# Attention followed by a gated MLP: natural token order for all batches at the gating step, one output store per token tile, and a divided last gating

## The chip, the cores and the metric

The kernel runs on one NeuronCore of a Trainium2 chip. The core has a matmul engine (TensorE, in profiles PE, with its weight loads as PEld), three engines for elementwise work (VectorE or DVE, ScalarE or ACT, GpSimd or POOL) and SyncE (SP), which here only issues DMAs. Each engine works through its own list of instructions in order and waits on semaphores for the others. The metric is the device time of one execution in microseconds (us). Before the change it was 246.58 us, the median of three runs (245.94 to 246.76).

## The reference

Eight batches of 384 tokens. First grouped-query attention: 16 query heads of 64 columns share 4 key and value heads. Its output, 384 x 1024 per batch, is the input of a gated MLP with a spatial part that mixes tokens. Cut to what matters:

```python
scores = matmul(q, k.T) / sqrt(64)           # per head, k and v repeated 4 times
x = softmax(scores) @ v                      # heads side by side: [8, 384, 1024]
h = maximum(x @ w_in, 0)                     # [8, 384, 1024]
u, v = h[..., :512], h[..., 512:]
v_n = (v - mean(v)) / sqrt(var(v) + 1e-6)    # per token
v_s = einsum('ts,bsd->btd', w_spatial, v_n) + b_spatial[None, :, None]
out = (u * v_s) @ w_out                      # [8, 384, 1024], float32
```

The product `u * v_s` is the gating; it is the step that the change touches.

## The kernel before

**Token orders.** Each batch has three token tiles (`NT = 3`) of 128. Queries are loaded so that one token is written as `c*12 + t*4 + r` (c of 32, t of 3, r of 4), and from the scores on the kernel's columns run in the order r, t, c within a tile; `units` (L254) turns the query columns with a rearrangement of its matmul's moving operand. So the attention output, and the MLP's activations after it, have their tokens in a permuted order: column `32*r + c` of tile t is token `c*12 + t*4 + r`. The spatial weights and bias are permuted to match when they are cast (`cast_spatial`, L527).

**Attention.** Per batch: `units` makes scores on PE and `exp` turns them into weights on ACT; `weigh` (L282) multiplies by v on PE, and DVE divides by the sums. A batch has six sets (query tile by head half), and a loop at the end of the kernel (L685 to L707) does one set per step. Keys, queries and attention outputs have to be transposed. In batches 0 and 1 PE does this; from batch 2 on SP issues DMA transposes: `k_send` and two `q_send` per batch (L237, L244), and one `x_send` per query tile (L324).

**MLP.** It is written as a generator, `gated` (L478), which the loop drains between attention's pieces (`pour`, L642), so that PE always has work. In a batch it makes `v_part` (v and its statistics), `norm` (POOL), `u_part`, then four times `s_part` (L416): three spatial matmuls into PSUM, a bias addition on DVE (`vs`, L433), and the gating product (`gT`). Output projection `o_part` (L450) of batch b stands in the generator of batch b+1: one call per token tile and half of 512 columns, four matmuls each, then a copy from PSUM to the tile `osb` on DVE or ACT. The last batch's six calls stand at the very end.

**Gating and stores before the change.** In batches 0 to 6, POOL multiplies in the permuted order (L435). In batch 7 the product is written with a stride, so that `gT` has the tokens in the order `token = 3*p + t` (L440): three on POOL, the fourth (`m == NM - 1`), which ends the wait of the last projection, on DVE. The stores follow: in batches 0 to 5 SP issues four DMAs after the third tile's second half, each from 32 partitions with all three tiles (L475); in batch 6 four per tile; in batch 7 one per tile and half from 128 partitions (L470). `osb` has two buffers of three tiles each.

**What sets the order.** Every engine's order is the order in which the program emits instructions (`manual_schedule`). Emission follows the loop: scores, part of the generator, the second half of the previous set's `weigh` with its `x_send`, more of the generator, the step's fixed tasks from `todo` (casts on POOL, `k_send`, `q_send`, loads), exponentials, and again the generator. SP therefore takes stores, transposes and loads strictly in that order, and each store waits at the head of SP's list until its copy is there. PSUM banks are given out by a planner that adds estimated costs (`bank`, `reads`); the change alters none of these costs.

**Set-up.** The spatial weights pass through a tile `early`, which takes a buffer of `osb`, and `ws16`, which takes one of `gT`. A `memset` on POOL (L581) overlaps both parts of `early`; SP's loads of the spatial weights and bias wait for it.

Of the kernel before, what the change touches and what calls it, by code (L numbers as in the profile page):

```python
# [9 lines left out]
FP32 = mybir.dt.float32  # L10
FP16 = mybir.dt.float16
AF = mybir.ActivationFunctionType
ALU = mybir.AluOpType
# [4 lines left out]
def kernel(  # L18
# [15 lines left out]
    P = 128  # L34
    B, HQ, S, D = q.shape
    HKV = k.shape[1]
    DM = moe_w_in.shape[0]
    DFF = moe_w_in.shape[1]
    DH = DFF // 2
    NT = S // P  # L40
    NK = DM // P
    NM = DH // P
    G = HQ // HKV
# [9 lines left out]
    cst = ctx.enter_context(tc.tile_pool(name="cst", bufs=1))  # L53
    ld = ctx.enter_context(tc.tile_pool(name="ld", bufs=2))
    att = ctx.enter_context(tc.tile_pool(name="att", bufs=2))
    moe = ctx.enter_context(tc.tile_pool(name="moe", bufs=2))
    small = ctx.enter_context(tc.tile_pool(name="small", bufs=4))
    ops = ctx.enter_context(tc.tile_pool(name="ops", bufs=2))
    ps = ctx.enter_context(tc.tile_pool(name="ps", bufs=1, space=PSUM))

    need = {AF.Exp, AF.Relu, AF.Copy, AF.Ln}
# [5 lines left out]
            name=nc.get_next_instruction_name(), act_func_set_id=set_id, ins=[], outs=[]  # L67
        )
    )
    pool, dve, act, sp = nc.gpsimd, nc.vector, nc.scalar, nc.sync  # L70
# [6 lines left out]
    def bank(shape, dtype, name):  # L77
        i = min(range(8), key=done.__getitem__)
        t = ps.tile(shape, dtype, name=name, tag=f"bank{i}")
        clock[nc.tensor] = max(clock[nc.tensor], done[i])  # L80
        done[i] = 1e12 + clock[nc.tensor]
        taken[name] = i
        return t

    def spend(ns):
        clock[nc.tensor] += ns

    def reads(eng, ns, name=None):
        clock[eng] = max(clock[eng], clock[nc.tensor] + 200.0) + ns
        if name:  # L90
            done[taken.pop(name)] = clock[eng]
# [60 lines left out]
    def load_w_in(half, lo, hi):  # L152
        cols = slice(half * DH, (half + 1) * DH)
        pool.dma_start(
            w_in16[:, lo:hi, cols],
            moe_w_in[lo * P : hi * P, cols].rearrange("(t p) f -> p t f", p=P),
        )
# [47 lines left out]
    def copy(eng, o, i, name):  # L205
        reads(eng, 200.0 + 0.52 * i.free_size(), name)
        (act.copy if eng is act else dve.tensor_copy)(o, i)  # L207
# [124 lines left out]
    v_r, v_n, mvs, uTs, gTs = {}, {}, {}, {}, {}  # L332
# [83 lines left out]
    def s_part(b, m):  # L416
        if m == 0:
            gTs[b] = moe.tile([P, NM, S], FP16, name=f"gT_{b}", tag="gT")
        psp = bank([P, 512], FP32, f"psp_{b}_{m}")
        for st in range(NT):  # L420
            nc.tensor.matmul(  # L421
                psp[:, 0:S],
                v_n[b, st][:, m * P : (m + 1) * P],
                wsT16[:, st, :],
                start=(st == 0),
                stop=(st == NT - 1),
            )
            spend(C384)
            if st < NT - 1:
                yield C384  # L430
        reads(dve, 470.0, f"psp_{b}_{m}")
        vs = moe.tile([P, S], FP32, name=f"vs_{b}_{m}", tag="vs", bufs=4)
        dve.tensor_tensor(vs, psp[:, 0:S], bias_bc, ALU.add)  # L433
        if b < B - 1:
            pool.tensor_tensor(gTs[b][:, m, :], vs, uTs[b][:, m, :], ALU.mult)  # L435
        else:
            def rows(x):
                return x.rearrange("p (o t c) -> p o t c", t=NT, o=G)

            (dve if m == NM - 1 else pool).tensor_tensor(  # L440
                gTs[b][:, m].rearrange("p (t c o) -> p o t c", t=NT, o=G),
                rows(vs),
                rows(uTs[b][:, m]),
                ALU.mult,
            )
        yield C384

    osbs = {}

    def o_part(b, tt, half):  # L450
        last = b == B - 1
        if tt == 0 and half == 0:
            osbs[b] = ops.tile([P, NT, DM], FP32, name=f"osb_{b}", tag="osb")
        po = bank([P, 512], FP32, f"po_{b}_{tt}_{half}")
        for m in range(NM):
            nc.tensor.matmul(  # L456
                po,
                gTs[b][:, m, tt * P : (tt + 1) * P],
                w_out16[:, m, half * 512 : (half + 1) * 512],
                start=(m == 0),  # L460
                stop=(m == NM - 1),
            )
            spend(C512)
            if m < NM - 1:
                yield C512
        cols = slice(half * 512, (half + 1) * 512)
        osb = osbs[b][:, tt, cols]
        copy(act if half and (last or tt == 1) else dve, osb, po, f"po_{b}_{tt}_{half}")
        if last:
            sp.dma_start(out[b].rearrange("(p t) d -> p t d", t=NT)[:, tt, cols], osb)  # L470
        elif half and (tt == NT - 1 or b == B - 2):
            ts = slice(tt, tt + 1) if b == B - 2 else slice(0, NT)
            rows = out[b].rearrange("(c t r) d -> r c t d", t=NT, r=G)
            for r in range(G):
                sp.dma_start(rows[r][:, ts], osbs[b][32 * r : 32 * r + 32, ts])  # L475
        yield C512

    def gated():  # L478
        for b in range(B):
            u0 = b * UNITS  # L480
            behind = [(b - 1, tt, half) for tt in range(NT) for half in range(2)] if b else []
            if b == 0:
                for st in range(NT):
                    yield ("from", 6 * st + 7)
                    yield from v_part(b, st, 0, 4)
                    yield ("from", 6 * st + 10)
                    yield from v_part(b, st, 4, 8)
            else:
                yield ("from", u0 + 12)
                yield from v_part(b, 0)  # L490
                for _ in range(1 if b == B - 1 else 2):
                    yield from o_part(*behind.pop(0))
                yield ("from", u0 + 18)
                yield from v_part(b, 1)
                yield ("from", u0 + 24)
                yield from v_part(b, 2)
# [9 lines left out]
            for m in range(NM):  # L506
                if behind:
                    yield from o_part(*behind.pop(0))
                yield from s_part(b, m)
            if behind:  # L510
                yield from o_part(*behind.pop(0))
# [2 lines left out]
                yield from o_part(B - 1, tt, half)  # L514


    early = ops.tile([P, NT, DM], FP32, name="early", tag="osb")
    ws32, b32 = early[:, :, 0:S], early[:, 0, S : 2 * S]
    ws16 = moe.tile([P, NT, NT, P], FP16, name="ws16", tag="gT")

    def load_spatial(eng):
        eng.dma_start(b32, moe_b_spatial.rearrange("(a s) -> a s", a=1).to_broadcast([P, S]))
        rows = moe_w_spatial.rearrange("(c t r) s -> r c t s", t=NT, r=G)
        for r in range(G):
            eng.dma_start(ws32[32 * r : 32 * r + 32], rows[r])
# [52 lines left out]
    load_v(1, pool)  # L578
    load_w_in(0, 0, 4)
    load_w_in(0, 4, 8)  # L580
    pool.memset(early[:, 0, S - 1 : S + 1], 0.0)  # L581
    load_spatial(sp)
    cast_k(1, pool)
    load_k(2, pool)
# [159 lines left out]
```

## Time and profile before

The profiled execution took 246.05 us; the runs' median is 246.58.

| | before |
|---|---|
| profiled execution, its own time | 246.05 us |
| span, first to last instruction | 244.3 us |
| granted TensorE clock, mean | 0.998 |
| PE busy | 234.9 us, 96% |
| ACT busy | 170.2 us, 70% |
| DVE busy | 144.9 us, 59% |
| POOL busy | 97.6 us, 40% |
| hardware DMA queue q1, share of 16 engines | 72.6% |
| output stores of L475, 384 KB | 24, median 6.3 us from issue to landing |
| output stores of L475, 128 KB | 12, median 2.1 us |
| output stores of L470, 256 KB | 6, median 2.8 us |
| gating on POOL, permuted order (L435) | 28, 912 ns (median) |
| gating on POOL, strided (L440) | 3, 1,059 ns |
| gating on DVE, strided (L440) | 1, 1,014 ns |

How to read it: "busy" is the time in which an engine executes; successive matmuls overlap and their ends are modelled, so a busy PE need not be at its peak rate, and two matmuls that follow one another start closer together than one lasts. `L456` is a line of the kernel. In a timeline, each line has start, duration, engine, line, operation and operands (out <- in), and in brackets how long the engine was idle before it and what ended that. SPq is SP's queue: the duration of a DMA there is that of its issue, not of its transfer. A waits line gives the waiting engine and line, who released it, then the total in us, the number of waits and the longest.

### The profile page before, as it was taken

The page shows a single profiled execution, that of the slowest core. Times are in us where ns is not written, and L with a number is a line of the kernel's source. Part 1 is how long each engine was busy: PE and PEld are TensorE (multiplying, and loading weights), DVE is VectorE, ACT ScalarE, POOL GpSimd, SP SyncE. Part 2 cuts the span into 40 slices and gives each one's busy share as a digit, 9 for nine tenths or more (in the row PEclk, how much of TensorE's full clock was granted, in tenths as well). Part 3 has the DMA queues.
Part 4 walks back from the last instruction along what each step waited for, and adds up shares of the span by engine and source line. Part 5 has one row for each costly group of instructions (what it writes and reads, how often), then busy time and mean ns, then how long its engine had stood idle before and what let it go on. Part 6 is the DMA issues. An engine that isn't in the chain of part 4 may idle for free.

```text
span 244.3 us, 5957 instructions
## 1 busy us (share of the span) xinstructions
PE 234.9 (96%) x2352; PEld 127.0 (52%) x2352; DVE 144.9 (59%) x377; ACT 170.2 (70%) x348; POOL 97.6 (40%) x137
## 2 busy tenths in 40 slices
PE   7899999999999999999999999899999999999992
PEld 6555565554555455555455455455455455545540
DVE  2677676567536765465844677266734767366371
ACT  2899977787898678968698776887597776402211
POOL 2677964545043900367024800466022400450520
PEclk9999999999999999999999999999999999999999
DMA  6999999992799999978999599987992297228267
GB/s 161 306 307 317 284 326 157 152 328 78 90 171 344 190 171 205 301 152 177 159 160 369 121 217 161 238 278 142 200 170 43 43 214 92 43 55 207 66 175 274
DMA packets 62411, 46.68 MB, mean 191 GB/s; under 512 B 45232, under 2 KB 54512, under 8 KB 62384
## 3 DMA queue, kind: packets, MB, share of 16 engines
q1 hardware_dynamic: 58560, 38.32, 72.6%
q0 software_dynamic: 3680, 7.87, 12.6%
q8 instruction: 18, 0.29, 0.5%
q10 hardware_dynamic: 144, 0.13, 0.3%
q14 instruction: 9, 0.07, 0.1%
HBM read 25.95 MB, written 12.58 MB: 158 GB/s over the span
## 4 chain that ended last, share of the span: by engine, by line
PE 74%; DMA 11%; SPq 8%; DVE 4%; issue 1%; ACT 0%; DVEq 0%
PE po L456 15%; PE pu L402 13%; PE pv L343 13%; PE sc L268 12%; PE av L288 12%; PE psp L421 7%; DMA wsT<-ws 5%; DMA qT<-q 5%; SPq L475 4%; SPq L239 3%; DMA k_None<-in_k_dram 1%; PE qps L229 1%; PE xps L320 1%; DVE x L303 1%; SPq L327 1%
## 5 line engine op out<-in xcount | busy, mean ns | idle before, releaser
L280 ACT ACTIVATE aT<-sc 128x512 f16<-128x512 f32 x288 | 147.7, 612 | 35.4 <-PE sc L268 34.7
L288 PEld LDWEIGHTS <-aT 128*128 128x128 f16 x1152 | 47.7, 97 | 17.7 <-issue 2.5
L288 PE MATMUL av<-v,aT 128*128 128x65 f16 x1152 | 51.7, 193 | 0.4 <-DVE osb L207 0.2
L343 PE MATMUL pv<-w_in,xt 128*128 128x512 f16 x192 | 51.3, 379 | 0.0
L456 PE MATMUL po<-w_out,gT 128*128 128x512 f16 x192 | 50.8, 379 | 0.4 <-DVE gT L440 0.4
L387 POOL TENSOR_SCALAR vn<-vr,rstd,nmr 128x512 f16<-128x512 f32 x24 | 18.1, 768 | 82.1 <-DVE nmr L382 60.3
L402 PE MATMUL pu<-xt,w_in 128*128 128x384 f16 x256 | 49.9, 326 | 0.0
L268 PE MATMUL sc<-qT,kT 64*128 64x512 f16 x288 | 42.7, 380 | 1.8 <-DMA qT<-q 1.2
L301 DVE RECIPROCAL r<-av 128x4 f32<-128x4 f32 x96 | 17.2, 179 | 43.4 <-PE av L288 43.2
L303 DVE TENSOR_TENSOR x<-av,r 128x256 f16<-128x256 f32 x96 | 40.8, 425 | 3.6 <-DVE r L301 0.4
L435 POOL TENSOR_TENSOR gT<-vs,uT 128x384 f16<-128x384 f32 x28 | 25.5, 914 | 29.5 <-DVE vs L433 15.0
L207 DVE COPY osb<-po 128x512 f32<-128x512 f32 x38 | 26.2, 689 | 17.4 <-PE po L456 17.2
L402 PEld LDWEIGHTS <-w_in 128*128 128x128 f16 x256 | 22.0, 97 | 17.1 <-issue 5.5
L413 ACT ACTIVATE uT<-pu 128x384 f16<-128x384 f32 x32 | 15.8, 494 | 17.1 <-PE pu L402 17.0
L456 PEld LDWEIGHTS <-gT 128*128 128x128 f16 x192 | 17.1, 97 | 17.9 <-issue 3.1
L268 PEld LDWEIGHTS <-kT 64*128 64x128 f16 x288 | 11.4, 94 | 26.2 <-issue 15.0
L343 PEld LDWEIGHTS <-xt 128*128 128x128 f16 x192 | 16.1, 97 | 17.3 <-issue 4.9
L194 POOL CAST q<-q 128x768 f16<-128x768 f32 x28 | 22.3, 827 | 6.8 <-DMA q<-in_q_dram 3.1
L421 PE MATMUL psp<-wsT,vn 128*128 128x384 f16 x96 | 22.3, 326 | 0.3 <-DMA wsT<-ws 0.3
L357 DVE TENSOR_SCALAR vr<-pv 128x512 f32<-128x512 f32 x24 | 16.4, 683 | 9.6 <-PE pv L343 9.5
L433 DVE TENSOR_TENSOR vs<-psp,bias_bc 128x384 f32<-128x384 f32 x32 | 17.6, 551 | 6.3 <-PE psp L421 4.8
L369 DVE BATCH_NORM_STATS2 stats<-vr 128x6 f32<-128x512 f32 x24 | 16.4, 685 | 0.1
(42 smaller groups left out, 102.8 us busy)
## 6 DMA issues: line engine op xcount, KB each, us to landing
out_dram<-osb SPq DMA_DIRECT2D x24, 384.0 KB, 6.3
q<-in_q_dram SPq DMA_DIRECT2D x10, 768.0 KB, 7.3
q<-in_q_dram POOLq DMA_DIRECT2D x4, 768.0 KB, 10.8
v_None<-in_v_dram SPq DMA_DIRECT2D x6, 384.0 KB, 4.6
w_in<-in_moe_w_in_dram POOLq DMA_DIRECT2D x4, 512.0 KB, 11.4
k_None<-in_k_dram SPq DMA_DIRECT2D x5, 384.0 KB, 4.0
out_dram<-osb SPq DMA_DIRECT2D x12, 128.0 KB, 2.1
out_dram<-osb SPq DMA_DIRECT2D x6, 256.0 KB, 2.8
```

The costliest lines, as they stand in the source:

```text
L194: eng.tensor_copy(t16[:, :, :, hh, :], src[:, hh])
L207: (act.copy if eng is act else dve.tensor_copy)(o, i)
L268: nc.tensor.matmul(sc, kTs[b][rows, j, kt * P : (kt + 1) * P], qTs[b, j][rows, qt].rearrange("p (r i c) -> p i r c", r=G, i=G), start=True ...
L280: act.activation(a, sc, AF.Exp, scale=scale)
L288: nc.tensor.matmul(av[:, i * (D + 1) : (i + 1) * (D + 1)], aT[:, kt, hh, i * P : (i + 1) * P], v1[b % 2][:, 2 * j + hh, kt, 0 : D + 1], st ...
L303: dve.tensor_tensor(x16s[b][:, qt, c : c + 256].rearrange("p (i d) -> p i d", i=G), o[:, :, 0:D], r.to_broadcast([P, G, D]), ALU.mult,)
L343: nc.tensor.matmul(pv, xts[b][:, kt, st * P : (st + 1) * P], w_in16[:, kt, DH:DFF], start=(kt == 0), stop=(kt == NK - 1),)
L387: pool.tensor_scalar(vn, v_r.pop((b, st)), rstd[:, st : st + 1], nmr[:, st : st + 1], op0=ALU.mult, op1=ALU.add,)
L402: nc.tensor.matmul(pu[:, 0:S], w_in16[:, kt, m * P : (m + 1) * P], xts[b][:, kt, :], start=(kt == 0), stop=(kt == NK - 1),)
L421: nc.tensor.matmul(psp[:, 0:S], v_n[b, st][:, m * P : (m + 1) * P], wsT16[:, st, :], start=(st == 0), stop=(st == NT - 1),)
L435: pool.tensor_tensor(gTs[b][:, m, :], vs, uTs[b][:, m, :], ALU.mult)
L456: nc.tensor.matmul(po, gTs[b][:, m, tt * P : (tt + 1) * P], w_out16[:, m, half * 512 : (half + 1) * 512], start=(m == 0), stop=(m == NM - 1),)
```

## The change

In every batch the gating product is now written in the strided form, so that `gT` has the natural order `token = 3*p + t` everywhere. With that, each token tile's output rows lie one per partition over all 128 partitions, and `o_part` issues one store per token tile (512 KB, rows of 4 KB) right after its second half, in batches 0 to 6 alike. Batch 7's stores stay one per tile and half. `osb` becomes one tile of `[128, 1024]` per token tile, with three buffers in all.

The last gating of batch 7 is divided: DVE writes the first token tile's 128 columns, POOL the other 256.

`early` is gone: the spatial weights, the bias and `ws16` get constant tiles of their own, and POOL has two memsets in place of one.

```diff
-    ops = ctx.enter_context(tc.tile_pool(name="ops", bufs=2))
+    ops = ctx.enter_context(tc.tile_pool(name="ops", bufs=3))
...
         dve.tensor_tensor(vs, psp[:, 0:S], bias_bc, ALU.add)
-        if b < B - 1:
-            pool.tensor_tensor(gTs[b][:, m, :], vs, uTs[b][:, m, :], ALU.mult)
+
+        gT = gTs[b][:, m].rearrange("p (t c o) -> p o t c", t=NT, o=G)
+        vs, uT = (x.rearrange("p (o t c) -> p o t c", t=NT, o=G) for x in (vs, uTs[b][:, m]))
+        if b < B - 1 or m < NM - 1:
+            pool.tensor_tensor(gT, vs, uT, ALU.mult)
         else:
-            def rows(x):
-                return x.rearrange("p (o t c) -> p o t c", t=NT, o=G)
-
-            (dve if m == NM - 1 else pool).tensor_tensor(
-                gTs[b][:, m].rearrange("p (t c o) -> p o t c", t=NT, o=G),
-                rows(vs),
-                rows(uTs[b][:, m]),
-                ALU.mult,
-            )
+            for eng, t in ((dve, slice(0, 1)), (pool, slice(1, NT))):
+                eng.tensor_tensor(gT[:, :, t], vs[:, :, t], uT[:, :, t], ALU.mult)
...
-        if tt == 0 and half == 0:
-            osbs[b] = ops.tile([P, NT, DM], FP32, name=f"osb_{b}", tag="osb")
+        if half == 0:
+            osbs[b, tt] = ops.tile([P, DM], FP32, name=f"osb_{b}_{tt}", tag="osb")
+        osb = osbs[b, tt]
...
-        osb = osbs[b][:, tt, cols]
-        copy(act if half and (last or tt == 1) else dve, osb, po, f"po_{b}_{tt}_{half}")
+        rows = out[b].rearrange("(p t) d -> p t d", t=NT)
+        copy(act if half and (last or tt == 1) else dve, osb[:, cols], po, f"po_{b}_{tt}_{half}")
         if last:
-            sp.dma_start(out[b].rearrange("(p t) d -> p t d", t=NT)[:, tt, cols], osb)
-        elif half and (tt == NT - 1 or b == B - 2):
-            ts = slice(tt, tt + 1) if b == B - 2 else slice(0, NT)
-            rows = out[b].rearrange("(c t r) d -> r c t d", t=NT, r=G)
-            for r in range(G):
-                sp.dma_start(rows[r][:, ts], osbs[b][32 * r : 32 * r + 32, ts])
+            sp.dma_start(rows[:, tt, cols], osb[:, cols])
+        elif half:
+            sp.dma_start(rows[:, tt, :], osb)
...
-    early = ops.tile([P, NT, DM], FP32, name="early", tag="osb")
-    ws32, b32 = early[:, :, 0:S], early[:, 0, S : 2 * S]
-    ws16 = moe.tile([P, NT, NT, P], FP16, name="ws16", tag="gT")
+    b32 = cst.tile([P, S], FP32, name="b32")
+    ws32 = cst.tile([P, NT, S], FP32, name="ws32")
+    ws16 = cst.tile([P, NT, NT, P], FP16, name="ws16")
...
-    pool.memset(early[:, 0, S - 1 : S + 1], 0.0)
+    pool.memset(b32[:, 0:1], 0.0)
+    pool.memset(ws32[:, 0, 0:1], 0.0)
```

## The prediction

> **What bounds the kernel now.** I read the busy table, PE's waits, the neighbourhood of each wait in the timeline, and last the DMA traffic of the tail.
>
> The busy table (engine, busy us, share of the span) and PE's own waits (us in total, times, longest):
>
> ```profile
> PE 234.9 (96%) x2352; PEld 127.0 (52%) x2352; DVE 144.9 (59%) x377; ACT 170.2 (70%) x348; POOL 97.6 (40%) x137
> ...
> PE sc L268 <- DMA qT<-q: 1.2, 2, 0.8
> ...
> PE po L456 <- DVE gT L440: 0.4, 1, 0.4
> ```
>
> PE is the bound; at a granted clock of 0.998 it can be helped only where it waits, and after its last matmul (235.22 + 4.71 = 239.93 of 244.3 us). Of its waits, the change can touch these two.
>
> First wait. The timeline of SP's queue, then of PE, around 139 to 154 us (start, us taken):
>
> ```profile
> 137.41 1.78 SPq L327 DMA_TRANSPOSE xt<-x  x1
> 139.29 4.60 SPq L475 DMA_DIRECT2D out_dram<-osb  x4
> 144.00 4.02 SPq L239 DMA_TRANSPOSE kT<-k  x1
> 148.13 4.11 SPq L246 DMA_TRANSPOSE qT<-q  x2
> ...
> 151.52 1.46 PE L402 MATMUL pu<-xt,w_in 128*128 128x384 f16 x8
> 153.79 0.39 PE L268 MATMUL sc<-qT,kT 64*128 64x512 f16 x2 [0.80 <-DMA qT<-q]
> ```
>
> Four stores hold SP for 4.6 us, the k transpose behind them takes 4.0 instead of the 1.2 to 1.5 it takes at 90.38 and 119.59, and q lands 5.6 us after its issue: PE waits. The same sequence stands 27.5 us later (wait 0.36 at 181.36).
>
> Second wait and the tail. DVE, PE and SP at the end, then the landing of the last batch's six stores:
>
> ```profile
> 234.15 1.01 DVE L440 TENSOR_TENSOR gT<-vs,uT 128x384 f16<-128x384 f32 x1
> 234.96 1.38 DVE L207 COPY osb<-po 128x512 f32<-128x512 f32 x2
> ...
> 233.17 1.67 PE L456 MATMUL po<-w_out,gT 128*128 128x512 f16 x7
> 235.22 4.71 PE L456 MATMUL po<-w_out,gT 128*128 128x512 f16 x21 [0.37 <-DVE gT L440]
> ...
> 229.55 7.86 SPq L475 DMA_DIRECT2D out_dram<-osb  x12
> 237.51 3.48 SPq L470 DMA_DIRECT2D out_dram<-osb  x6
> ...
> L470 SPq DMA_DIRECT2D out_dram<-osb x6: 376/400/581, 237.5 to 240.6; - x6
> DMA to landing us min/median/max: 2.5/2.8/3.0
> ```
>
> And the traffic of three windows: 218.1 to 222 (only 32-partition stores), 236.5 to 239 (batch 6's last 32-partition stores, then the first of batch 7) and 239.2 to 243 (only 128-partition stores):
>
> ```profile
> DMA packets 208, 0.80 MB, mean 206 GB/s; under 512 B 16, under 2 KB 16, under 8 KB 206
> ...
> DMA packets 223, 0.59 MB, mean 236 GB/s; under 512 B 63, under 2 KB 63, under 8 KB 223
> ...
> DMA packets 790, 1.42 MB, mean 374 GB/s; under 512 B 96, under 2 KB 96, under 8 KB 790
> ```
>
> The reader should see that stores from 32 partitions move 206 GB/s and stores from 128 partitions 374, and that from 236.5 to 243 the queue never empties: the last store, issued at 240.57, lands 2.8 us later, behind the ones before it.
>
> **The change, part by part.**
>
> *Stores of batches 0 to 5.* 24 issues of 384 KB become 18 of 512 KB. Their price on the engines that issue and move them is unknown, so bounds: issue between 0.40 us (128 rows of 2 KB, L470) and 0.67 (the first of a burst of four), take 0.55; transfer between 0.52 MB / 206 = 2.5 us and 0.52 / 374 = 1.4, take 1.4, because the row with 128 partitions is the nearer one. Where each goes in SP's order follows from PE's order: the third tile's store stays where the four were, behind an x transpose and ahead of the k transpose; the second tile's falls between two x transposes, where SP waits for DVE (5.9 us before 137.41) and its copy (ACT, done at 133.63) is long over; the first tile's comes after or between the two q transposes and ahead of an x transpose. Queued behind its wait there are an x transpose, needed about a batch later, and loads for two batches ahead; only batch 1's, near 87, falls ahead of k and q transposes, whose data are wanted at 100.9. So ahead of the k transpose 4.6 us and 1.57 MB become 0.55 us and 0.52 MB. From 139.29: store to 139.85, k transpose 1.2 to 1.5 to 141.4, first q transpose issued there, landing in 4.0 to 5.6: 147 at the latest, wanted at 152.8. Both waits go, with 5 us to spare; even 206 GB/s would cost only 1.1 of it. What each is worth: the eighth pu starts at 152.98 - 0.33 = 152.65, the next matmul could start one step (0.16) later, 152.82; 153.79 is 0.97 late, of which about 0.10 is the usual change to a score matmul (148.13 to 148.39 is 0.26). So 0.87; likewise 181.36 - (179.70 + 1.30 - 0.33 + 0.16) - 0.10 = 0.43. **Minus 1.3 us.** Nothing is late next there: the batches that start at 100.9 and 125.8 run the same work and show no such wait.
>
> *Gating written with a stride, batches 0 to 6.* 28 POOL instructions go from 912 to 1,059 ns (the three strided ones of L440): 4.1 us of POOL, which is 40% busy. Tightest cover: batch 6's last gating, 217.54 to 218.45, would end at 218.60, and its weights load at 218.69. The casts behind gatings in POOL's queue come 0.15 to 0.3 later; the one for the second q ends at 139.33, and its transpose would not be wanted before 142.5. Cost 0; without the cover at most 0.15 per batch.
>
> *Last gating divided.* It delays PE: the matmul before the wait starts at 233.17 + 1.67 - 0.38 = 234.46, the next could at 234.68 and does at 235.22: 0.54 late. DVE keeps 128 of 384 columns. Lower bound a third of 1,014, 338 ns; upper: DVE's plain products (256 columns 425, 384 columns 551) give 172 + 0.98 per column, so 298 ns, plus all of the 463 that the strided one costs more as if fixed, 760. I take the excess as per column: 298 + 154 = 452. Ready at 234.60, the 0.05 until PE follows included before 234.68: **minus 0.54** (0.26 at 760 ns). POOL's 256 columns, two thirds of 1,059 = 0.71, from 234.17 to 234.9, are wanted first by the second token tile at about 236.4: hidden.
>
> *Tail stores.* Batch 6's 12 issues become 3. Its last tile is copied 0.5 earlier, so its store goes at about 235.2 (235.70 now), moves in 1.4 instead of 2.2 us, and SP is free for batch 7's first store at once, where now four issues run until 237.42. All 2.1 MB at 374 GB/s take 5.6 us instead of 6.4 from the first packet on. The last store then hardly queues. Its landing by rows: 128 KB stores land in 1.9 at least, 0.35 to 0.64 of it transfer, so 1.4 fixed; 256 KB take 0.7 more: 2.1 in place of 2.8. **Minus 0.7** (bounds 0 and 0.8).
>
> *Three output buffers of one tile.* The copy of batch 7's third tile (239.10 now, 238.56 then) must wait for batch 6's third store: issued 235.2, 1.4 fixed + 1.4 = 238.0. Cost 0; at 206 GB/s it lands at 239.1, and the last issue comes 0.2 later.
>
> *Own tiles for the spatial weights.* A second memset, at most 0.155 us, ahead of loads that are issued from 16.60 to 19.63 and land in 7.1 and 8.8 (medians); POOL uses them from 28.71 and 29.51. Cost 0; with the cover gone 0.15, at the matmul that waits 0.3 for wsT.
>
> Sum: -1.3 - 0.54 - 0.7 = -2.5 us against the profiled execution: span 244.3 to 241.8, its own time 246.05 (span plus 1.75) to 243.5. The median of the runs, 246.58, is 0.53 above that execution; carried to it, **244.1 us**.
>
> **The rivals.**
>
> *POOL's piece holds up DVE's.* Both halves have two SBUF inputs. If they cannot run at once and POOL starts first, DVE's 128 columns begin at 234.17 + 0.71 and are ready at 235.33, 0.16 after today's 235.17: PE loses 0.16 instead of winning 0.54. 244.8 us. For it: nothing in the trace overlaps two such instructions, and POOL starts 0.08 to 0.14 after vs, DVE 0.10, nearly a tie. Against: DVE's L433 takes its 0.55 beside POOL's L440 all the same (230.79 beside 230.07), but it reads PSUM. If DVE starts first, POOL ends at 235.3, which is still hidden. The Trainium skill, page "SBUF — State Buffer", section "Who interferes with whom", says that such a VectorE instruction and a GpSimd one that reads SBUF exclude each other for their whole length; by that rule the halves never overlap, and the sum would be 244.1 or 244.8 by who starts first. No run here shows it yet. Chance 0.2.
>
> *The 128-partition store of whole rows moves only 206 GB/s.* Then batch 6's last one moves in 2.5 instead of 2.2 us, from 0.5 earlier, and batch 7's six follow without a gap as now: the end wins 0.2 instead of 1.24, 245.1. For it: its rows are 4 KB like those of the slow ones. Against: 374 with 128 partitions. Chance 0.1.
>
> *The transposes stay late,* held by something that the stores hide now (a cast on POOL, the release of a buffer): then 1.3 is missing, 245.4. Against: at 119.59 to 124.3 the same three need 4.7 us of SP in all. Chance 0.12.
>
> *Slower: too few output buffers.* Batch 7's third copy waits for batch 6's third store. If that lands at L, the copy takes 0.7, two issues 0.4 each follow, and the last lands 2.1 later: L + 3.4. That beats all that the middle wins (243.37 + 1.3) from L = 241.3, a landing of 6.1 us. 384 KB stores have taken up to 8.3 in this trace: L = 243.5, 248.8 us. Against: those ran among transposes, and none is left here. Chance 0.08.
>
> **Numbers.** Forecast 0.5. Range 243.2 to 245.8: below, the forecast's bounds (0.1 more in the tail, 0.1 in the landing of the waits) and the runs' spread (245.94 to 246.76); above, the transposes staying late with some of that spread. 0.3% (0.74 us) is about what a measurement tells from no change. Forecast, the first two rivals and most of the third are faster by more: 0.84; same 0.07; slower 0.09.
>
> **What would show it.** SP: one store of about 0.55 us ahead of each k transpose, k transposes of 1.2 to 1.5, and no wait of PE for qT. DVE's strided product near 0.45 us, beginning beside POOL's and not after it, and PE's 28 last matmuls without a gap. Traffic near 374 GB/s in every store, last landing about 2.1. It is wrong if PE waits for qT again, if a copy waits for out_dram near the end, or if POOL's longer products appear among PE's releasers.

## The result and the profile after

The changed kernel took 243.77 us (median of six runs), the kernel before 246.36 in six runs; the ratio is 0.9891 with a 95% interval of 0.9874 to 0.9908, so it is 1.1% faster. One of the six, 247.67 us, was slower than the rest at a lower granted clock (0.993) and is not in the ratio. Forecast were 244.1 us and a range of 243.2 to 245.8. The profiled execution took 243.88 us with a span of 241.8, the span that the sum had given. Outside the span lie 2.0 us, against 1.75 before.

The busy table after, and under it all of PE's waits (total us, times, longest):

```profile
PE 234.9 (97%) x2352; PEld 127.0 (53%) x2352; DVE 143.9 (60%) x377; ACT 169.8 (70%) x348; POOL 100.8 (42%) x139
...
PE idle L552 <- POOL ident masks.py:199: 1.4, 1, 1.4
PE qps L229 <- DVE q L197: 0.5, 1, 0.5
PE sc L268 <- DVE qT L207: 0.4, 2, 0.3
```

PE's work is the same 234.9 us. What is gone are its waits for qT and for the last gating, and two smaller ones that stood in the same list before:

```profile
PE psp L421 <- DMA wsT<-ws: 0.3, 1, 0.3
PE av L288 <- DVE osb L207: 0.2, 1, 0.2
```

POOL has 3.2 us more.

SP's queue at the place where the first wait arose, then PE where the score matmul had waited 0.80 us:

```profile
137.18 1.90 SPq L327 DMA_TRANSPOSE xt<-x  x1
139.17 0.53 SPq L469 DMA_DIRECT2D out_dram<-osb  x1
139.81 1.49 SPq L239 DMA_TRANSPOSE kT<-k  x1
141.39 3.35 SPq L246 DMA_TRANSPOSE qT<-q  x2
144.83 0.86 SPq L469 DMA_DIRECT2D out_dram<-osb  x1
...
151.29 1.46 PE L402 MATMUL pu<-xt,w_in 128*128 128x384 f16 x8
152.69 0.82 PE L268 MATMUL sc<-qT,kT 64*128 64x512 f16 x6
```

One store of 0.53 us stands ahead of the k transpose, which takes 1.49; the first q transpose goes out 6.7 us earlier than before, and the score matmul starts without a wait.

The tail: the last gating in its two parts, PE behind it, SP, and the landing of the six last stores:

```profile
232.62 0.45 DVE L441 TENSOR_TENSOR gT<-vs,uT 128x128 f16<-128x128 f32 x1
232.66 0.88 POOL L441 TENSOR_TENSOR gT<-vs,uT 128x256 f16<-128x256 f32 x1 [0.33 <-DVE vs L433]
...
231.64 6.21 PE L453 MATMUL po<-w_out,gT 128*128 128x512 f16 x28
...
233.61 0.33 SPq L469 DMA_DIRECT2D out_dram<-osb  x1
234.29 4.54 SPq L467 DMA_DIRECT2D out_dram<-osb  x6
...
L467 SPq DMA_DIRECT2D out_dram<-osb x6: 332/332/333, 234.3 to 238.5; - x6
DMA to landing us min/median/max: 2.0/2.2/2.7
```

All 28 matmuls of the last projections run without a gap. The last store, issued at 238.50, lands after 2.0 us; the prediction had taken 2.1 for one that does not queue.

To see where the 2.4 us came from, I cut each span at points that all kernels have: the first score matmul of batches 2, 4 and 7, the last spatial matmul, the start of the last projection matmul, the issue of the last store, the moment SP sees it landed, the end. Durations in us, from the start times in the traces:

| stage | before | after | difference |
|---|---|---|---|
| set-up, batches 0 and 1 | 51.56 | 51.60 | +0.04 |
| batches 2, 3 | 49.32 | 49.12 | -0.20 |
| batches 4 to 6 | 80.49 | 79.10 | -1.39 |
| batch 7 to the last spatial matmul | 51.65 | 51.66 | +0.01 |
| to the last projection matmul | 6.54 | 5.99 | -0.55 |
| to the issue of the last store | 1.03 | 1.03 | 0 |
| to its landing, seen by SP | 2.80 | 2.03 | -0.77 |
| to the end | 0.90 | 1.32 | +0.42 |

In the profiles of the experiments the stages from batch 2 to the last spatial matmul repeat within 0.1 us where the kernels do not differ there; the first one varies from 50.6 to 52.6 us without a relation to the edits that I could see. That is the scatter of the runs, and the reason why effects of half a microsecond are read below from the stages and not from the medians alone.

### The profile page after: what moved, and what is told of

It reads as the page before. It is cut to its first block, busy times and chain, and to the rows that moved or that the text cites. A ratio compares the mean times of both kernels' runs of the same rounds, so it can differ in the third digit from the quotient of the medians.

```text
span 241.8 us, 5961 instructions
## 1 busy us (share of the span) xinstructions
PE 234.9 (97%) x2352; PEld 127.0 (53%) x2352; DVE 143.9 (60%) x377; ACT 169.8 (70%) x348; POOL 100.8 (42%) x139
## 4 chain that ended last, share of the span: by engine, by line
PE 94%; DVE 3%; issue 0%; ACT 0%; POOL 0%; POOLq 0%
PE pu L402 18%; PE po L453 18%; PE pv L343 17%; PE sc L268 16%; PE av L288 15%; PE psp L421 7%; PE idle L552 2%; PE xps L320 1%; PE qps L229 1%; DVE x L303 1%; DVE vr L357 1%; PE kps L215 1%; DVE qT L207 1%; DVE q L197 0%; DVE r L301 0%
## 5 line engine op out<-in xcount | busy, mean ns | idle before, releaser
L453 PE MATMUL po<-w_out,gT 128*128 128x512 f16 x192 | 50.6, 379 | 0.0
L438 POOL TENSOR_TENSOR gT<-vs,uT 128x384 f16<-128x384 f32 x31 | 32.5, 1059 | 33.4 <-DVE vs L433 16.9
L268 PEld LDWEIGHTS <-kT 64*128 64x128 f16 x288 | 10.9, 94 | 24.9 <-issue 13.9
L433 DVE TENSOR_TENSOR vs<-psp,bias_bc 128x384 f32<-128x384 f32 x32 | 17.6, 552 | 6.5 <-PE psp L421 6.3
```

Of the source, the lines that this page charges most:

```text
L268: nc.tensor.matmul(sc, kTs[b][rows, j, kt * P : (kt + 1) * P], qTs[b, j][rows, qt].rearrange("p (r i c) -> p i r c", r=G, i=G), start=True ...
L438: pool.tensor_tensor(gT, vs, uT, ALU.mult)
L453: nc.tensor.matmul(po, gTs[b][:, m, tt * P : (tt + 1) * P], w_out16[:, m, half * 512 : (half + 1) * 512], start=(m == 0), stop=(m == NM - 1),)
```

## The experiments

**1. The division undone.** The changed kernel, DVE doing the whole last gating:

```diff
-            for eng, t in ((dve, slice(0, 1)), (pool, slice(1, NT))):
+            for eng, t in ((dve, slice(0, NT)),):
```

> The changed kernel with the last gating undivided again: DVE writes all 384 columns. Theory (the division is worth its 0.54 us because the last store no longer queues): the product takes about 1.01 us, PE's last projection shows a gap again whose matmul comes 0.5 us late, the last landing moves by as much, 0.45 to 0.6 us more than the changed kernel (243.8), about 244.3. Rival (the end is set by the queue of output stores, not by PE): the gap returns but the last landing does not move, 243.8.

Measured: 244.26 us (six runs, 244.09 to 244.58), 0.49 more than the changed kernel. PE's gap is back:

```profile
PE po L453 <- DVE gT L441: 0.4, 1, 0.4
```

The two kernels did not run at the same time, and their ratios to the kernel before, 0.9899 (0.9861 to 0.9936) here and 0.9891, do not tell them apart. The stages do: the one to the last projection matmul is 6.54 again, 0.55 more, and landing and end are as in the changed kernel (2.03 and 1.34). The theory holds: with the queue gone, PE's half microsecond reaches the end in full.

**2. The division alone.** The kernel before, with the last gating of batch 7 divided:

```diff
-            (dve if m == NM - 1 else pool).tensor_tensor(
+            parts = ((pool, slice(0, NT)),)
+            if m == NM - 1:
+                parts = ((dve, slice(0, 1)), (pool, slice(1, NT)))
+            for eng, t in parts:
...
```

> The kernel before with nothing but the last gating of batch 7 divided between DVE (first token tile) and POOL. Theory: PE's gap of 0.37 us before the last projection goes; batch 6's last stores start 0.5 us earlier and the queue of stores moves with them, so 0.5 us less than before (246.4), about 245.9; the last store still lands 2.8 us after its issue and the two waits for qT (0.8 and 0.4) stay. Rival (the queue of stores alone sets the end): PE ends 0.5 us earlier, but the last landing only 0 to 0.2, 246.2 to 246.4.

Measured: 245.55 us in twelve runs beside 246.48 of before, ratio 0.9956 (0.9932 to 0.9979). The stage to the last projection matmul is 5.99, the last store needs 2.78 us to land as before, and the waits for qT stay:

```profile
PE sc L268 <- DMA qT<-q: 1.2, 2, 0.8
```

So the queue of stores moves forward with PE and does not eat the gain; the rival falls.

**3. The tail's stores alone.** The kernel before, with batch 6 in the natural order and one store per token tile:

```diff
-        if b < B - 1:
+        if b < B - 2:
...
+        elif half and b == B - 2:
+            rows = out[b].rearrange("(p t) d -> p t d", t=NT)
+            sp.dma_start(rows[:, tt, :], osbs[b][:, tt, :])
```

> The kernel before with nothing but batch 6 changed: its gating strided, one store of 512 KB from 128 partitions per token tile in place of four of 128 KB. Theory (the queue at the end is worth 0.7 us): the last store lands 2.0 to 2.2 us after its issue in place of 2.8, both waits for qT and the gap at the last projection stay; 0.6 to 0.8 us less than before, about 245.7. Rival (a store of whole rows from 128 partitions is as slow as the old ones, or the last landing is a fixed time): 2.8 us as before, 246.4.

Measured: 245.64 us in twelve runs, ratio 0.9965 (0.9942 to 0.9988). PE's gap and the waits for qT are still there; the last store lands 2.05 us after its issue, 0.75 less than before, and 0.95 us of closing follow. The queue at the end is worth what the step had given.

**4. The slow burst, later.** The kernel before, its stores unchanged, those of batches 0 to 4 issued after the next batch's first token tile:

```diff
-        elif half and (tt == NT - 1 or b == B - 2):
...
+            if tt == 0 and 0 < b < B - 2:
+                jobs.append((b - 1, slice(0, NT)))
```

> The kernel before, its stores as they are (four of 384 KB from 32 partitions), but those of batches 0 to 4 issued one projection later, behind the q transposes in SP's order. Theory (the waits come from what stands ahead of the k and q transposes): both waits of PE for qT (0.8 and 0.4 us) vanish although each burst still takes 4.6 us of SP and moves 206 GB/s; 1.3 us less than before, about 245.1; loads and x transposes behind it come some 4 us later, unnoticed. Rival (the waits come from the slow stores wherever they stand, or the late loads make POOL's casts late): waits remain or new ones of PE for xt or qT appear, 246.4 or more.

Measured: 250.8 us, ratio 1.013 (1.0075 to 1.0186): slower, and my expectation was wrong. PE's waits, SP's queue around 90 and 124 us, and the windows view (window, its length, busy us of PE, PEld, DVE, ACT, POOL with instructions, granted clock, DMA share, GB/s) of this kernel:

```profile
PE sc L268 <- DMA qT<-q: 3.9, 2, 3.4
...
88.56 6.01 SPq L482 DMA_DIRECT2D out_dram<-osb  x4
94.67 4.03 SPq L239 DMA_TRANSPOSE kT<-k  x1
98.80 4.88 SPq L246 DMA_TRANSPOSE qT<-q  x2
...
121.92 1.29 SPq L246 DMA_TRANSPOSE qT<-q  x1
123.76 4.72 SPq L482 DMA_DIRECT2D out_dram<-osb  x4
128.58 4.61 SPq L246 DMA_TRANSPOSE qT<-q  x1
...
100.00:105.00 5.00, 1.58 (x13) 0.72 (x11) 0.61 (x2) 1.30 (x3) 0.00 (x0) 0.87 1.27 166
105.00:110.00 5.00, 5.00 (x34) 2.29 (x29) 1.85 (x4) 3.04 (x6) 0.76 (x1) 0.50 0.99 239
110.00:115.00 5.00, 5.00 (x53) 2.77 (x51) 2.87 (x8) 3.63 (x7) 1.98 (x5) 0.95 1.05 343
115.00:140.00 25.00, 24.52 (x250) 12.83 (x249) 14.68 (x39) 18.90 (x40) 8.54 (x12) 1.00 0.91 162
```

One projection later is behind the q transposes only for those of batches 6 and 7 (bursts at 151.44 and 178.09), and there the waits are gone. For those of batch 4 the burst comes to stand right ahead of the k transpose, for those of batch 5 between the two q transposes, and just there PE now waits 3.4 and 0.5 us. So the place of a slow burst decides, as the theory says, but the edit had not put it where I meant. The rest of the loss is the clock: during the long wait the granted clock fell to 0.50, at 103.7, and stayed there for 6.8 us; from 110.5 on it was 1.00 again. The span of this execution is 5.5 us longer than before: 2.7 of them are more waiting for qT (3.9 against 1.2), and 2.7 are the same matmuls taking longer (PE is busy for 237.6 us in place of 234.9).

**5. The slow burst, truly behind.** To repair experiment 4, the bursts of batches 0 to 3 became a fixed task right behind the second q transpose:

```diff
         at(u0 - 8, q_send, b, 1)
+        if b > 3:
+            at(u0 - 8, store, b - 4, slice(0, NT))
```

> The kernel before with its stores as they are (four of 384 KB from 32 partitions), but those of batches 0 to 3 issued as one of the fixed tasks, right behind the second q transpose of the batch that they stood ahead of. Theory (what stands ahead of the k and q transposes makes the waits; the store's rate does not): both waits of PE for qT (0.8 and 0.4 us) are gone and no others come, 1.3 us less than before, 245.1 at 246.4 of before. Rival (slow bursts make PE wait wherever they stand, as in the run with the late burst): waits for qT or xt stay, 246.4 or more.

Measured: 246.36 us in twelve runs, ratio 1.0025 (0.9999 to 1.0051): no gain. No wait for qT is left, but another has come. PE's waits, then POOL and PE near 113 us in this kernel:

```profile
PE po L456 <- POOL gT L435: 1.8, 1, 1.8
...
109.40 0.95 POOL L178 CAST k<-k_None 128x384 f16<-128x384 f32 x2 [3.96 <-issue]
110.31 1.78 POOL L435 TENSOR_TENSOR gT<-vs,uT 128x384 f16<-128x384 f32 x2
113.22 1.59 POOL L194 CAST q<-q 128x768 f16<-128x768 f32 x2 [1.12 <-issue]
114.77 0.91 POOL L435 TENSOR_TENSOR gT<-vs,uT 128x384 f16<-128x384 f32 x1
...
115.73 0.39 PE L456 MATMUL po<-w_out,gT 128*128 128x512 f16 x1 [1.85 <-POOL gT L435]
...
116.20:119.60 3.40, 3.40 (x22) 1.40 (x19) 1.14 (x3) 2.95 (x6) 1.79 (x3) 0.50 1.09 139
```

The load of k that stood behind the burst was issued at 103.89 instead of 97.08. POOL waits for it before its cast: the timeline gives no releaser for the 3.96 us (`issue`), but the load lands 5.4 us after its issue, at 109.3, and the cast starts at 109.40. The first load of q behind it, issued at 105.74, lands at 113.1, just ahead of the cast at 113.22. Gatings stand behind casts in POOL's order, and the projection waits for the gating. So moving the burst removes the waits for qT, as the theory said, but a slow burst in one piece takes about as much elsewhere, which the theory had ruled out ("unnoticed", I had written of the loads in experiment 4). The profiled execution took 248.85 us; in it the granted clock was 0.50 from 116.2 to 119.6, just after the wait (the last line above, in the form of experiment 4's windows). Another run took 248.78 us, and these two have a mean clock of 0.991, the other ten 0.997 to 1.000 and 245.3 to 246.74 us.

**6. The new rate, the old place.** The changed kernel, with the stores of batches 0 to 5 held back until the third tile, and with a fourth output buffer:

```diff
-    ops = ctx.enter_context(tc.tile_pool(name="ops", bufs=3))
+    ops = ctx.enter_context(tc.tile_pool(name="ops", bufs=4))
...
-        elif half:
-            sp.dma_start(rows[:, tt, :], osb)
+        elif half and b == B - 2:
+            sp.dma_start(rows[:, tt, :], osb)
+        elif half and tt == NT - 1:
+            for t in range(NT):
+                sp.dma_start(rows[:, t, :], osbs[b, t])
```

> The changed kernel with the stores of batches 0 to 5 held back until the third token tile, three of 512 KB in a row where the four stood (with a fourth output buffer, so that no copy waits for them). Theory (the rate from 128 partitions alone would do): 1.57 MB at 374 GB/s take 4.2 us in place of 7.6, the k transpose starts on the engines near 144.5, q lands near 149 to 150 and is wanted at 152.8: no wait for qT, 243.8 like the changed kernel. Rival (spreading the stores is what removes the waits): PE waits for qT again by 0.3 to 0.8 us in one or two batches, 244.3 to 245.0.

Measured: 244.37 us in four runs, ratio 0.993 (0.9906 to 0.9954). PE has no wait for qT. SP's queue:

```profile
139.92 1.96 SPq L472 DMA_DIRECT2D out_dram<-osb  x3
141.99 2.55 SPq L239 DMA_TRANSPOSE kT<-k  x1
144.63 3.48 SPq L246 DMA_TRANSPOSE qT<-q  x2
```

Three whole tiles from 128 partitions hold SP for 2.0 us instead of 4.6, and the q transposes go out in time. From the first score matmul of batch 5 to that of batch 6, and from there to that of batch 7, the stretches in which the two waits lay, this kernel takes 27.15 and 27.14 us: as in the changed kernel (27.16 and 27.13), against 28.02 and 27.57 before. So the faster stores remove both waits in full, even in the old place. The stage of batches 4 to 6 is 79.45 us all the same, against 79.10 in the changed kernel; the 0.35 lie in batch 4, in one score matmul that starts late, at 106.0. The profile puts it down to no wait, but it starts 0.05 us after the end of DVE's bias addition `vs` (L433, 105.41 to 105.97), and that addition, counted from the batch's first score matmul, runs about 0.35 us later than in the changed kernel. Whether the burst makes it late is not shown.

**7. The new place, the old partitions.** The changed kernel, every whole-row store cut into four from 32 partitions:

```diff
-            sp.dma_start(rows[:, tt, :], osb)
+            for r in range(G):
+                pr = slice(32 * r, 32 * r + 32)
+                sp.dma_start(rows[pr, tt, :], osb[pr, :])
```

> The changed kernel with every whole-row store cut into four of 128 KB from 32 partitions each, in the same places. Theory: four issues of 0.4 us and 0.52 MB at 206 to 240 GB/s ahead of the k transpose still leave q 3 us in hand, so no wait for qT; at the end the queue is back, the last store lands 2.6 to 2.8 us after its issue: 0.6 to 0.9 us more than the changed kernel, 244.4 to 244.7. Rival (only the number of bytes and their place count, not the partitions): 243.8.

Measured: 243.74 us in five runs, the median of the changed kernel; taken by itself it would speak for the rival. The stages say otherwise. In the middle there is no wait for qT, batches 4 to 6 take 79.12, and the two stretches of experiment 6 take 27.15 and 27.14 again:

```profile
139.62 2.36 SPq L471 DMA_DIRECT2D out_dram<-osb  x4
142.09 1.24 SPq L239 DMA_TRANSPOSE kT<-k  x1
143.43 3.64 SPq L246 DMA_TRANSPOSE qT<-q  x2
```

There the theory holds: stores from 32 partitions remove both waits too, once they are cut by token tile and spread over the new places. At the end the last store is issued 1.41 us after the start of the last matmul instead of 1.03 and lands 2.56 after that instead of 2.03: 0.91 us later, near the upper end of what was expected. But the end follows 0.89 us after the landing instead of 1.32, which takes 0.43 back. The net 0.5 us is lost in the scatter of five runs (243.18 to 245.2). The edit changes the number of DMAs together with their partitions, so what each of the two adds at the end is not shown. Experiments 9 and 10 are about those 0.43.

**8. POOL's piece alone, and who comes first.** Three kernels ask whether the two halves of the divided gating exclude each other. First, POOL's 256 columns measured with no DVE product beside them, by cutting the three earlier gatings of batch 7 in the same way:

```diff
-            pool.tensor_tensor(gT, vs, uT, ALU.mult)
+            cuts = (slice(0, NT),) if b < B - 1 else (slice(1, NT), slice(0, 1))
+            for t in cuts:
+                pool.tensor_tensor(gT[:, :, t], vs[:, :, t], uT[:, :, t], ALU.mult)
```

> The changed kernel with the first three gatings of batch 7 cut in two on POOL: 256 columns, then 128, with no DVE product from two SBUF operands beside them. It measures POOL's 256 columns by themselves. If DVE's piece held POOL's up in the changed kernel (879 ns there), they take about 710 ns alone, two thirds of 1,059; if not, about 880 alone as well. The time should be that of the changed kernel within 0.3 us.

Then two tiny memsets ahead of DVE's piece (`dve.memset(hold[:, i : i + 1], 0.0)`, twice):

> The changed kernel with two tiny memsets on DVE ahead of its piece of the last gating, so that POOL's piece starts first. If the two exclude each other: DVE's product ends only 0.45 us after POOL's (879 ns), PE's last projection shows a gap of 0.6 to 0.8 us and the end is as much later. If they do not: DVE's product still takes 0.45 us, only 0.1 to 0.2 us later than in the changed kernel, and PE's gap is 0.15 us at most.

Then one memset of 512 columns in the same place:

> The changed kernel with a memset of 512 columns on DVE ahead of its piece of the last gating, so that POOL's piece starts clearly first (by 0.2 us or more). If the two exclude each other: DVE's product ends 0.45 us after POOL's end (POOL 0.77 alone), or is shown longer by that wait, 1.2 to 1.3 us after the end of vs, and PE's last projection has a gap of 0.7 to 1.0 us. If they run side by side: DVE's product takes 0.45 to 0.55 us from its start, 0.3 to 0.5 us later than in the changed kernel, PE's gap 0.2 to 0.5 us.

Measured, one run each: 243.66, 243.7 and 244.16 us. The groups by form of the first kernel, and the timeline of the third:

```profile
L440 POOL TENSOR_TENSOR gT<-vs,uT 128x256 f16<-128x256 f32 x3 | 2.3, 766 | 2.9 <-DVE vs L433 2.9
L443 POOL TENSOR_TENSOR gT<-vs,uT 128x256 f16<-128x256 f32 x1 | 0.9, 876 | 0.3 <-DVE vs L433 0.3
...
232.68 0.48 DVE L441 MEMSET hold<- 128x512 f32 x1
232.76 1.16 POOL L443 TENSOR_TENSOR gT<-vs,uT 128x256 f16<-128x256 f32 x1 [0.33 <-DVE vs L433]
233.07 0.38 DVE L443 TENSOR_TENSOR gT<-vs,uT 128x128 f16<-128x128 f32 x1
```

Alone, POOL's piece takes 0.77 us, beside DVE's 0.88. The tiny memsets changed nothing: DVE's product still began 0.04 us ahead of POOL's, so that run did not put the question. With the long memset POOL was first by 0.31 us; DVE's product then ran inside POOL's, in 0.38 us, and it was POOL's that became 0.39 longer. So something gets in POOL's way, and the one that pays is POOL and not DVE, whichever starts first. How much of the 0.39 is the product's doing is not shown: the memset ran beside POOL's piece as well, for 0.4 us. PE's gap in that kernel is 0.25 us, which the later start of DVE's piece accounts for. The rival that POOL's piece holds up DVE's has no ground here. The rule of the Trainium skill (page "SBUF — State Buffer", section "Who interferes with whom"), by which the second to issue is blocked until the first has finished, does not describe these two: DVE's came second and was not blocked, and when POOL's came second, 0.04 us later, it lost 0.11 us and not the 0.41 that were left of DVE's product.

**9. and 10. The closing checks.** After its last store, SP checks the semaphores of all engines and DMAs one by one. In the changed kernel the stage from landing to end is 0.42 us longer than before. A store in the middle, behind which SP idles, was cut into eight, so that the last store gets another of the eight semaphores that DMAs take in turn:

```diff
-            sp.dma_start(rows[:, tt, :], osb)
+            cuts = 8 if (b, tt) == (4, 1) else 1
+            for i in range(cuts):
+                pr = slice(i * P // cuts, (i + 1) * P // cuts)
+                sp.dma_start(rows[pr, tt, :], osb[pr, :])
```

> The changed kernel with one store in the middle (batch 4, second tile, where SP idles for 3.4 us behind it) cut into eight of 16 partitions, so seven more DMAs. In the changed kernel SP's closing checks begin with the last store's semaphore and then take seven more of 0.065 us each after the landing; before, the last store's came last of all. DMAs take their semaphores from eight in turn, so seven more put the last store's at the end of the checks again. Theory (the closing checks give back 0.45 us of what the tail won): from the last landing to the end 0.9 us in place of 1.35, PE and all stages as in the changed kernel, 0.4 us less than the changed kernel on the same chip. Rival (the checks run beside something else that ends the kernel): no difference.

Beside it, on the same chip, the changed kernel again:

> The changed kernel again, as the measure for the run with seven more DMAs: 243.8 us, 1.0 to 1.2% less than before; closing checks of 1.35 us after the last landing. Both theories expect the same.

Measured: 243.01 us (four runs, 242.91 to 243.22), ratio 0.9879 (0.9856 to 0.9902); the changed kernel again 243.32 us (six runs, 242.7 to 243.85), ratio 0.9893 (0.987 to 0.9915). SP's waits in its closing checks (total us, times, longest), in the kernel before, in the changed kernel and in the one with seven more DMAs:

```profile
SPq L739 <- DMA out_dram<-osb: 1.9, 3, 0.6
```

```profile
SPq L734 <- DMA out_dram<-osb: 1.6, 1, 1.6
```

```profile
SPq L737 <- DMA out_dram<-osb: 1.2, 2, 0.7
```

In the changed kernel the first check of a DMA is the one that waits longest, for the very last store; the other seven follow at 0.06 us each (0.065 in the expectation), though all they ask about is over. In the kernel before, and with seven more DMAs, the last store's check comes last. From landing to end it is 0.89 us instead of 1.34 in the repeated run, and all other stages agree within 0.03 but the set-up. So the mechanism is shown in the trace, 0.45 us. What lies outside the span goes the same way: a run's time less its span is 1.74 to 1.82 us in the four runs of this kernel and 1.74 to 1.85 in the runs of before beside them, but 1.90 to 2.15 in the six of the changed kernel. No profile shows what these 0.2 us are. By the medians this kernel is 0.3 us faster than the changed one, but the intervals overlap; it is the fastest version that was run.

## Why the prediction was right

*What bounds the kernel.* Right: PE's busy time did not move by a tenth, and the gain lies in its waits and in the tail.

*Stores, k and q transposes: -1.3.* Right, also in its parts: the stretch from batch 5's first score matmul to batch 6's became 0.86 us shorter and the next one 0.44, where 0.87 and 0.43 were forecast. The last 0.10 of the stage's 1.39 lie in batch 4 and were not in the sum. Ahead of the transposes of batch 6 the order of events was the one forecast: 0.53 us of SP (0.55 forecast), k transpose 1.49 (1.2 to 1.5), first q transpose at 141.39 (141.4); it was much the same for batch 7. Not met was one store of about 0.55 us ahead of every k transpose: for batch 4 the store took 1.74 us and the k transpose 1.62, for batch 5 two stores took 5.01 together and the k transpose 2.10. PE waited there neither before nor after. As for the reason, the change does two things at once: the stores move faster, and less of them stands ahead of the transposes. Experiments 6 and 7 show that either of the two is enough to remove both waits; the prediction's remark that even 206 GB/s would leave q in time was right. No run has neither of the two with the rest of the change; that the waits would then be back is argued from the queue before. Experiment 5 shows what does not do: a slow burst moved in one piece makes PE wait elsewhere.

*The 128-partition store at 374 GB/s.* Nearly right: the tail's stores, batch 6's last one among them, moved 350 GB/s on average from 234.4 to 240.4 us, and from 180 us on whole-row stores land in 2.6 us in the median (1.4 fixed and 1.4 transfer were taken). Experiment 7 shows the price of four stores from 32 partitions in its place at the end.

*Strided gating: 0.* Right. POOL's 31 products take 1,059 ns each, as taken from L440; POOL's busy time rose by 3.2 us, and its products are in none of PE's waits.

*The last gating divided: -0.54.* Right: -0.55. DVE's 128 columns took 447 ns where 452 was taken between 338 and 760. POOL's piece was too small in the sum (0.71 by two thirds; 0.77 alone and 0.88 beside DVE), without effect.

*The tail: -0.7.* The mechanism was right, -0.77 to the landing, but as a term of the sum it was mis-sized: 0.42 came back in SP's closing checks, an item between landing and end that I had taken as the same in both. The net is -0.35.

*Three output buffers, own tiles: 0.* Right: no copy waits for a store in the changed kernel. The set-up stage differs by 0.04 us.

That the span was met to 0.1 us is thus partly luck. The tail gave 0.35 less than forecast, the middle 0.09 more, and batches 2 and 3 gave 0.20 that were not in the sum: before, a weighting matmul at 85.9 waited for DVE's copy of `osb` (0.2 us), and that wait is gone. The step from the span to a time had luck too: 1.75 us outside the span were taken and 2.03 measured, so the profiled execution took 243.88 us where 243.5 were forecast, but the median of the runs, put 0.53 above it, lay 0.11 below it.

## What to carry to other kernels

A PE-bound kernel is still worth searching for single waits of a microsecond; where one ends with a transfer, the first thing to ask is what stands ahead of that transfer in its queue and how long it holds it. Moving slow traffic in one piece to another place in an in-order queue only helps if what then stands behind it has slack. Here, making it fast where it stood, or cutting it up and spreading it, each removed both waits. At the end of a kernel, count what follows the last landing as a term of its own.

## What the runs showed that was not expected

- SP's closing checks cost 0.06 us each and their order matters: 0.9 us from landing to end when the last store's check is last, 1.3 when it is the first of the DMAs'. Outside the span the second order goes with 0.2 us more.
- While PE waited 3.4 us, its granted clock fell to 0.50 and stayed there for 6.8 us, against 1.00 in the same part of the kernel before. After a wait of 1.85 us in another kernel it was 0.50 for 3.4 us in the profiled execution; by the mean clocks, only one of the other eleven runs of that kernel, 248.78 us with 0.991, had the like.
- A DVE product that began 0.31 us after a POOL product from the same tiles took 0.38 us all the same, and the POOL product, which had a DVE memset beside it as well, 0.39 us longer than alone.
